# Fewer zero products around the last expert products, a first store on another queue, ten split rows for twelve

## The chip, the core and the metric

One core of a Trainium2 chip runs the whole kernel. The metric is the device time of one execution in microseconds; the figure of the kernel before is the median of 13 runs. The profile is one execution, seen by the hardware profiler: it gives the start and length of every instruction on TensorE (PE, with its weight loads as PEld), VectorE (DVE), ScalarE (ACT), GpSimd (POOL) and SyncE (SP), the packets of the 16 DMA engines, and the clock that TensorE was granted.

## What is computed

Two operations follow each other. Attention over q, k, v of shape (4, 8, 768, 64), where each head is either full causal or causal with 4 sink positions and a window of 64; its output, laid out as x of shape (3072, 512), goes into a soft mixture of experts (8 experts with 4 slots each):

```
x = attention(q, k, v).transpose(0, 2, 1, 3).reshape(3072, 512)
logits = x @ phi                                   # 3072 x 32
d = exp(logits) normalised over tokens;  c = exp(logits) normalised over slots
slot_input = d.T @ x                               # 32 x 512
slot_out[e] = relu(slot_input[e] @ w1[e]) @ w2[e]  # w1: 512 x 1024, w2: 1024 x 512, for 8 experts
out = c @ slot_out                                 # 3072 x 512, f32
```

The combine product at the end needs every expert's slot output, so no row of the output can be made before the last w2 is in.

## The kernel before

**The attention** is one loop over 16 pairs of heads (`for n in range(NP)`, L324). For pair n the loop issues six chunks of scores with their exponentials (`scores`, L158 to L170), transposes q and k of pair n+1 on TensorE (`transposes`, L139) and copies them out of PSUM (`evac`, q on DVE at L146, k on ACT at L149), and multiplies the probabilities of pair n-1 by v (`pvmm`, L191). The order on each engine is the order of the source, written out by hand; nothing is reordered by a scheduler.

**The loads** all go through one GpSimd queue, in source order: q and k (L110), v (L116), w1 and w2 (L130), and at the end w2 of expert 5 (L405), the left half of columns of w2 of expert 6 (L407), and then, in one loop at L421, w2 of expert 7 left, of expert 6 right and of expert 7 right. They convert f32 in HBM to bf16 in SBUF.

**The tail** (from L427) runs the experts. `second(e, xs)` (L508 to L515) multiplies the hidden rows of expert e by w2[e] for the left half (x = 0) or the right half (x = 1) of the 512 output columns, into two PSUM tiles `sp[0]` and `sp[1]`; that is eight products per half and expert. TensorE's order is: the 24 small products of the row sums (L532), `second(5)`, `second(6)` and `second(7)` for the left half, the left half of `slot_out` copied by DVE (L563), the left half of the first NL = 12 rows of the output, `second(6)` and `second(7)` for the right half, the right half of `slot_out` (L568), then twelve rows in full width and the right half of the first twelve. Row r here means one output row of each of the 128 partitions. `product` (L545 to L551) makes one such row: a product into one of four PSUM buffers, then a scaled copy to SBUF, by DVE for even r (L551) and by ACT for odd r (L549).

**The stores.** `half_rows` (L553 to L560) stores groups of finished half rows; the left ones go out on the GpSimd queue in groups of 2, 2, 4 and 4. The full rows are stored by SP at L576 (groups of 1, 1, 2, 4, 4), the right half rows by SP at L560 (4, 4, 4). SP has issued nothing since L253 when the stores begin. A half row is 1 KB per partition, a full row 2 KB.

**Zero products.** `keep_busy(t, count)` (L266 to L268) issues products of a tile of zeros into a bank that nobody reads: 128 x 512 each. There are 9 at the very start (L271), 2 after each of the first transposes (L299), 2 in each of three places of the first pair, and at the end 1 (L472), 4 (L534), 4 (L536), 4 (L538) and 3 (L566); some at L425 and L450 besides.

Of the kernel before, what the change touches and what calls it, by code (L numbers as in the profile page):

```python
# [10 lines left out]
F32 = mybir.dt.float32  # L11
# [27 lines left out]
def kernel(  # L39
# [13 lines left out]
    nc = tc.nc  # L53
    P = 128
# [3 lines left out]
    NE, DM, F = moe_w1.shape  # L58
# [16 lines left out]
    def single(shape, dt, name, tag=None):  # L75
        return singles.tile(shape, dt, name=name, tag=tag or name)
# [29 lines left out]
    def load_qk(pairs, which):  # L106
        b, h, c = pairs[0] // 4, 2 * (pairs[0] % 4), 2 * len(pairs)
        src, d = (q, qraw) if which == "q" else (k, kraw)
        t = raw.tile([P, len(pairs), S], BF16, tag="r" + which, name="r" + which)
        nc.gpsimd.dma_start(t, src[b, h:h + c].rearrange("(y h) (p s) d -> (h p) y (s d)", h=2, s=12))  # L110
        for x, n in enumerate(pairs):
            d[n] = t[:, x]

    def load_v(m):
        b, h = m // 2, 4 * (m % 2)
        nc.gpsimd.dma_start(vbs[m % 3].rearrange("p h j d -> p (h j) d")[:, :, :D],  # L116
                            v[b, h:h + 4].rearrange("h (j p) d -> p (h j) d", p=P))
# [8 lines left out]
    def w_load(upto):  # L126
        while wi[0] < min(upto, 2 * NE - 3):
            e = wi[0] % NE
            dst, src = ((w1s, w1v), (w2s, w2v))[wi[0] // NE]
            nc.gpsimd.dma_start(dst[e], src[e])  # L130
            wi[0] += 1

    def transposes(n, which):
        src = (qraw if which == "q" else kraw)[n]
        tp = trp.tile([P, 12, 64], BF16, tag="tr", name="tp" + which)
        for s in range(12):
            for hh in range(2):
                po = slice(64 * hh, 64 * hh + 64)
                nc.tensor.transpose(tp[po, s, :], src[po, 64 * s:64 * s + 64], ident[po, po])  # L139
        return tp  # L140

    def evac(n, which, tp):
        dst = qkT.tile([P, S], BF16, tag="T" + which, name="T" + which)
        o, i = dst.rearrange("c (p s) -> c p s", s=12), tp.rearrange("c s p -> c p s")
        if which == "q":
            nc.vector.tensor_copy(o, i)  # L146
            qT[n] = dst
        else:
            nc.scalar.copy(o, i)  # L149
            kT[n] = dst  # L150
# [7 lines left out]
    def scores(n, c):  # L158
        o, ln, parts = CHUNKS[c]
        sc = scp.tile([P, 2, 512], F32, tag="sc", name="sc")  # L160
        at = 0
        for j, i0, cnt in parts:
            for hh in range(2):
                po = 64 * hh
                nc.tensor.matmul(sc[:, hh, at:at + 128 * cnt], kT[n][po:po + 64, j * 128:(j + 1) * 128],  # L165
                                 qT[n][po:po + 64, i0 * 128:(i0 + cnt) * 128], start=True, stop=True)
            at += 128 * cnt
        if c == 0:
            pT[n] = ptp.tile([P, 2, NPT], BF16, tag="pT", name="pT")
        nc.scalar.activation(pT[n][:, :, o:o + ln], sc[:, :, :ln], ACT.Exp, scale=scale)  # L170
# [50 lines left out]
    def logits_exp(b):  # L221
        nc.scalar.activation(expT[:, b], lgs[b][:96], ACT.Exp, accum_out=colpart[:, b:b + 1])  # L222
# [43 lines left out]
    def keep_busy(t, count):  # L266
        for _ in range(count):
            nc.tensor.matmul(t, zero[:, :P], zero, start=True, stop=True)  # L268

    idle = pvp.tile([P, 512], F32, tag="pv", name="idle")  # L270
    keep_busy(idle, 9)  # L271
    V.tensor_single_scalar(ident, diff[:, :P], 0.0, op=ALU.is_equal)
    one_row = single([1, P], BF16, "one_row")
    V.memset(one_row, 1.0)
# [19 lines left out]
    def head_mask(h):  # L294
        V.tensor_scalar(msk[:, h], grade, thr[:, h:h + 1], None, op0=ALU.is_ge)

    for which in ("k", "q"):
        evac(0, which, transposes(0, which))
        keep_busy(idle, 2)  # L299
    for h in range(2):  # L300
        head_mask(h)
    def far_mask(n):
# [21 lines left out]
    for n in range(NP):  # L324
        if n == 0:
            load_qk([2], "q")
            load_qk([2], "k")
            load_v(1)
        elif n == 1:
            load_qk([3], "q")  # L330
            load_qk([3], "k")
        elif n == 2 or (n % 2 == 1 and n < 12):
            m = 2 if n == 2 else (n + 3) // 2
            load_qk([2 * m, 2 * m + 1], "q")
            load_qk([2 * m, 2 * m + 1], "k")
            load_v(m)
        w_load(1 + 5 * (n + 1) // 8)
        if n == 0:
            nc.gpsimd.dma_start(phi, moe_phi.rearrange("(do di) s -> di do s", di=P))
        b, r = n // 4 - 1, n % 4  # L340
        last = n - 1

        scores(n, 0)
        if n == 0:
            keep_busy(idle, 2)
        if n >= 1:
            for i in range(3):
                pvmm(last, i)
        if b >= 0 and r == 2:
            logits_mm(b, (0, 1, 2, 3))  # L350

        scores(n, 1)
        if b >= 0 and r == 2:
            logits_exp(b)
        if n >= 1:
            norm(last, 0)
        if n + 1 < NP:
            tq = transposes(n + 1, "q")
            evac(n + 1, "q", tq)
        mask(n, 0)  # L360
        if b >= 0 and r == 3:
            exp_tokens(b)

        scores(n, 2)
        if n == 0:
            keep_busy(idle, 2)
        if n >= 1:
            pvmm(last, 3)
        if n >= 2:
            x_transpose(n - 2)  # L370
        mask(n, 1)

        scores(n, 3)
        if n + 1 < NP:
            tk = transposes(n + 1, "k")
        mask(n, 2)

        scores(n, 4)
        if n == 0:
            keep_busy(idle, 2)  # L380
        if n + 1 < NP:
            evac(n + 1, "k", tk)
        if n >= 1:
            pvmm(last, 4)
        vfar(n)

        scores(n, 5)
        if n >= 1:
            pvmm(last, 5)
            norm(last, 1)  # L390
        if b >= 0 and r == 3:
            dispatch_mm(b)
            slot_sum(b)
        if n < 3:
            far_mask(n + 1)
            for h in (2 * n + 2, 2 * n + 3):
                head_mask(h)
        elif n == 3:
            setup_late()
# [22 lines left out]
    idle = scp.tile([P, 512], F32, tag="sc", name="idle")  # L422
# [44 lines left out]
    cs = bank(1, (P, 1))  # L467
# [1 line left out]
    rcol = small.tile([P, 1], F32, tag="rc", name="rcol")  # L469
    V.reciprocal(rcol, cs)  # L470
    V.tensor_scalar(emask, emask, rcol, None, op0=ALU.mult)
    keep_busy(idle, 1)  # L472
    hs = []
    for e4 in range(2):
        t = xp.tile([P, 2, 512], BF16, tag="xb", name="hs")
# [30 lines left out]
    idle = spt[1][:, 1]  # L506
# [24 lines left out]
        er.append(e)  # L531
        nc.tensor.matmul(rp[:, r:r + 1], e[:ES], ones[:ES], start=True, stop=True)  # L532
    V.reciprocal(rrow, rp)
    keep_busy(idle, 4)  # L534
    second(5, spread=True)
    keep_busy(idle, 4)  # L536
    second(6, (0,), spread=True)
    keep_busy(idle, 4)  # L538
    second(7, (0,), spread=True)


    NL = 12
    ov = out.rearrange("(p r) d -> p r d", r=24)

    def product(r, o, cs, t):  # L545
        op = bank(t, (P, cs.stop - cs.start))
        nc.tensor.matmul(op, er[r], slot_out[:, cs], start=True, stop=True)  # L547
        if r % 2:
            nc.scalar.activation(o, op, ACT.Copy, scale=rrow[:, r:r + 1])  # L549
        else:  # L550
            V.tensor_scalar(o, op, rrow[:, r:r + 1], None, op0=ALU.mult)  # L551

    def half_rows(cs, t0, groups, banks, eng):  # L553
        ots = [single([P, n, 256], F32, f"oh{t0 + x}", tag=f"w1_{t0 + x}") for x, n in enumerate((8, NL - 8))]
        r = 0
        for rows in groups:
            for _ in range(rows):
                product(r, ots[r // 8][:, r % 8], cs, banks[r % len(banks)])
                r += 1
            eng.dma_start(ov[:, r - rows:r, cs], ots[(r - 1) // 8][:, (r - rows) % 8:(r - 1) % 8 + 1])  # L560

    left, right, full = slice(0, 256), slice(256, 512), slice(0, 512)
    V.tensor_copy(slot_out[:, left], sp[0])  # L563
    half_rows(left, 0, (2, 2, 4, 4), (1, 2), nc.gpsimd)
    second(6, (1,), spread=True)
    keep_busy(idle, 3)  # L566
    second(7, (1,), spread=True)
    V.tensor_copy(slot_out[:, right], sp[1])  # L568
    r = NL
    for t, groups in enumerate(((1, 1, 2), (4,), (4,))):  # L570
        ot = single([P, 4, DM], F32, f"ot{t}", tag=f"w1_{4 + t}")
        for rows in groups:
            for _ in range(rows):
                product(r, ot[:, r % 4], full, (1, 2)[r % 2])
                r += 1
            nc.sync.dma_start(ov[:, r - rows:r, :], ot[:, (r - rows) % 4:(r - 1) % 4 + 1])  # L576
    half_rows(right, 2, (4, 4, 4), (1, 2), nc.sync)


# [33 lines left out]
```

## Time and profile before

| what | value |
|---|---|
| time, median of 13 runs | 160.6 us (158.83 to 163.75) |
| the profiled execution's own time | 160.6 us |
| its span, first to last instruction | 158.8 us |
| outside the span | 1.8 us |
| mean granted TensorE clock | 0.952 |
| busy: PE, DVE, ACT, POOL | 122.6, 107.7, 108.6, 40.5 us |
| read from HBM, written to HBM | 52.49 MB, 6.29 MB |
| last product (L547) ends, last scaled copy (L549) ends | 146.8, 147.3 us |

Times inside a profile are counted from the span's start. In the table of windows each row is one stretch of time: its length, the busy time of PE, PEld, DVE, ACT and POOL with the number of instructions in brackets, the granted TensorE clock (1.00 is full), the busy share of the DMA engines, and GB/s. These GB/s count bytes as they land: a weight is 4 bytes in HBM and 2 in SBUF. "DMA to landing" runs from the start of the issuing instruction to the moment when its semaphore says that all is there.

### The profile page before, as it was taken

To read this page: it belongs to the slowest core of one execution; us is meant where nothing else is said; L and a number is where in the kernel's file an instruction comes from. 1 tells how busy PE (TensorE), PEld (TensorE's weight loads), DVE (VectorE), ACT (ScalarE), POOL (GpSimd) and SP (SyncE) were. 2 spreads that over 40 slices of the span, in tenths; PEclk is the share of its full clock that TensorE was granted. 3 is DMA by queue.
4 is the path that set the end of the run, shared out by engine and by line. 5 is a ranking of instruction groups with operands and counts; after the bars stand their busy time and mean duration, and the time that the engine had idled before them with its cause. 6 is when DMAs were issued, how large, how long until landed. Compare 5 with 4: busy or idle time off the path is not lost. (4 is left out here: it accounts for less than half of the span.)

```text
span 158.8 us, 5124 instructions
## 1 busy us (share of the span) xinstructions
PE 122.6 (77%) x2272; PEld 75.1 (47%) x2272; DVE 107.7 (68%) x249; ACT 108.6 (68%) x147; POOL 40.5 (25%) x57
## 2 busy tenths in 40 slices
PE   6947679597697799897979977978879999778000
PEld 2422456365465565565655655655544753444000
DVE  6268599888986978977878977868655300769000
ACT  3248799769799989999998999897124310659100
POOL 7584153601330440340392000003600000420000
PEclk9999999969999999999999999999999987999955
DMA  3999999999999999999999999999999999299993
GB/s 51 161 175 202 172 224 197 195 191 187 218 215 200 188 217 199 188 212 200 195 211 194 203 206 229 204 225 204 227 208 216 189 200 166 68 302 398 396 344 101
DMA packets 38744, 32.87 MB, mean 207 GB/s; under 512 B 26050, under 2 KB 35778, under 8 KB 36802
## 3 DMA queue, kind: packets, MB, share of 16 engines
q0 software_dynamic: 36416, 27.82, 111.7%
q1 hardware_dynamic: 2306, 4.72, 8.0%
q8 instruction: 18, 0.29, 0.7%
q14 instruction: 4, 0.03, 0.1%
HBM read 52.49 MB, written 6.29 MB: 370 GB/s over the span
## 5 line engine op out<-in xcount | busy, mean ns | idle before, releaser
L170 ACT ACTIVATE pT<-sc 128x1024 bf16<-128x1024 f32 (+1 forms) x96 | 83.5, 924 | 10.5 <-PE sc L165 9.9
L165 PE MATMUL sc<-Tq,Tk 64*128 64x256 bf16 (+3 forms) x320 | 35.4, 283 | 12.1 <-ACT Tk L149 11.0
L191 PEld LDWEIGHTS <-pT 128*128 128x128 bf16 x672 | 24.3, 98 | 11.5 <-issue 6.9
L182 DVE TENSOR_TENSOR pT<-pT,msk 128x1024 bf16<-128x1024 bf16 (+1 forms) x48 | 29.2, 639 | 0.0
L191 PE MATMUL pv<-vb,pT 128*128 128x65 bf16 x352 | 26.9, 194 | 0.3 <-DVE xb L200 0.3
L191 PE MATMUL pv<-vf,pT 128*128 128x65 bf16 x320 | 24.8, 196 | 0.0
L165 PEld LDWEIGHTS <-Tk 64*128 64x128 bf16 x320 | 10.6, 94 | 21.7 <-ACT Tk L149 13.7
L146 DVE COPY Tq<-tpq 128x768 bf16<-128x768 bf16 x16 | 15.3, 957 | 7.2 <-PE tpq L139 6.9
L200 DVE TENSOR_TENSOR xb<-pv,rs 128x384 bf16<-128x384 f32 x32 | 17.8, 558 | 1.1
L149 ACT COPY Tk<-tpk 128x768 bf16<-128x768 bf16 x16 | 12.9, 809 | 4.1 <-PE tpk L139 4.1
L110 POOL DMA_DIRECT2D rq<-in_q_dram x10 | 6.4, 639 | 35.9 <-PE sc L165 34.2
L199 DVE RECIPROCAL rs<-pv 128x6 f32<-128x6 f32 x32 | 6.2, 194 | 10.2 <-PE pv L191 10.2
L116 POOL DMA_DIRECT2D vb<-in_v_dram x8 | 11.6, 1452 | 3.5 <-PE pv L191 3.5
L139 PE MATMUL tpq<-ident,rq 64*64 64x64 bf16 x384 | 9.2, 196 | 4.1 <-DMA rq<-in_q_dram 4.1
L139 PEld LDWEIGHTS <-rq 64*64 64x64 bf16 x384 | 7.4, 111 | 8.3 <-DMA rq<-in_q_dram 4.9
L549 ACT ACTIVATE oh<-bank,rrow 128x256 f32<-128x256 f32 x12 | 5.2, 472 | 8.6 <-PE bank L547 8.5
L139 PE MATMUL tpk<-ident,rk 64*64 64x64 bf16 x384 | 9.6, 200 | 1.0 <-DVE Tq L146 1.0
L139 PEld LDWEIGHTS <-rk 64*64 64x64 bf16 x384 | 7.9, 114 | 4.6 <-issue 4.6
L268 PE MATMUL idle<-zero 128*128 128x512 bf16 x24 | 9.1, 496 | 1.2 <-DVE zero L264 1.2
L208 PE MATMUL tpx<-ident,xb 128*128 128x128 bf16 x96 | 8.4, 224 | 2.0 <-ACT expT L222 1.1
L547 PE MATMUL bank<-slot_out,expR 128*128 128x256 bf16 (+1 forms) x36 | 7.8, 306 | 2.3 <-DVE slot_out L568 0.5
L209 DVE COPY xT<-tpx 128x768 bf16<-128x768 bf16 (+1 forms) x17 | 9.0, 529 | 0.7 <-PE tpx L208 0.6
(92 smaller groups left out, 127.1 us busy)
## 6 DMA issues: line engine op xcount, KB each, us to landing
w<-in_moe_w_dram POOLq DMA_DIRECT2D x13, 1024.0 KB, 18.3
w<-in_moe_w_dram POOLq DMA_DIRECT2D x6, 512.0 KB, 18.9
vb<-in_v_dram POOLq DMA_DIRECT2D x8, 384.0 KB, 13.2
rq<-in_q_dram POOLq DMA_DIRECT2D x6, 384.0 KB, 12.0
rk<-in_k_dram POOLq DMA_DIRECT2D x6, 384.0 KB, 12.2
out_dram<-ot SPq DMA_DIRECT2D x2, 1024.0 KB, 8.0
out_dram<-oh SPq DMA_DIRECT2D x3, 512.0 KB, 9.1
out_dram<-oh POOLq DMA_DIRECT2D x2, 512.0 KB, 4.3
```

Source lines behind the costliest of these rows:

```text
L116: nc.gpsimd.dma_start(vbs[m % 3].rearrange("p h j d -> p (h j) d")[:, :, :D], v[b, h:h + 4].rearrange("h (j p) d -> p (h j) d", p=P))
L139: nc.tensor.transpose(tp[po, s, :], src[po, 64 * s:64 * s + 64], ident[po, po])
L146: nc.vector.tensor_copy(o, i)
L149: nc.scalar.copy(o, i)
L165: nc.tensor.matmul(sc[:, hh, at:at + 128 * cnt], kT[n][po:po + 64, j * 128:(j + 1) * 128], qT[n][po:po + 64, i0 * 128:(i0 + cnt) * 128], s ...
L170: nc.scalar.activation(pT[n][:, :, o:o + ln], sc[:, :, :ln], ACT.Exp, scale=scale)
L182: nc.vector.tensor_mul(x, x, m)
L191: nc.tensor.matmul(pv[n][:, i % 3, hh, :], pT[n][:, hh, o:o + 128], vv[:, hh, j, :D + 1], start=(j == 0), stop=(j == i))
L200: nc.vector.tensor_mul(xb[b][:, 3 * half:3 * half + 3, h * D:(h + 2) * D].rearrange("p i (h d) -> p i h d", h=2), pv[n][:, :, :, :64], rs. ...
L208: nc.tensor.transpose(tp[:, i * 128:(i + 1) * 128], xb[b][:, i, hp * 128:(hp + 1) * 128], ident)
L209: nc.vector.tensor_copy(xT[:, hp, i0 * 128:i1 * 128], tp[:, i0 * 128:i1 * 128])
L268: nc.tensor.matmul(t, zero[:, :P], zero, start=True, stop=True)
```

## The change

- At the front: 7 zero products for 9, and none after the first transposes or inside the first pair (10 fewer there; the ones at L425 and L450 stay).
- At the end: the 1 of L472 and the 4 of L534 go; the 4 of L536 stay; of the 4 of L538 one stays; the 3 of L566, between the right halves of experts 6 and 7, go.
- The first of the left stores is issued by SP, the others by GpSimd as before.
- NL is 10. The left groups are 2, 2, 4, 2; the full-width rows are 14, in groups of 1, 1, 2, 4, 4, 2; the right groups are 4, 4, 2.

```diff
-    keep_busy(idle, 9)
+    keep_busy(idle, 7)
...
         evac(0, which, transposes(0, which))
-        keep_busy(idle, 2)
...
-        if n == 0:
-            keep_busy(idle, 2)
...
     V.tensor_scalar(emask, emask, rcol, None, op0=ALU.mult)
-    keep_busy(idle, 1)
...
     V.reciprocal(rrow, rp)
-    keep_busy(idle, 4)
     second(5, spread=True)
     keep_busy(idle, 4)
     second(6, (0,), spread=True)
-    keep_busy(idle, 4)
+    keep_busy(idle, 1)
     second(7, (0,), spread=True)
...
-    NL = 12
+    NL = 10
...
-    def half_rows(cs, t0, groups, banks, eng):
+    def half_rows(cs, t0, groups, banks, engs):
...
-            eng.dma_start(ov[:, r - rows:r, cs], ots[(r - 1) // 8][:, (r - rows) % 8:(r - 1) % 8 + 1])
+            engs[min(r > 2, len(engs) - 1)].dma_start(ov[:, r - rows:r, cs], ots[(r - 1) // 8][:, (r - rows) % 8:(r - 1) % 8 + 1])
...
-    half_rows(left, 0, (2, 2, 4, 4), (1, 2), nc.gpsimd)
+    half_rows(left, 0, (2, 2, 4, 2), (1, 2), (nc.sync, nc.gpsimd))
     second(6, (1,), spread=True)
-    keep_busy(idle, 3)
     second(7, (1,), spread=True)
...
-    for t, groups in enumerate(((1, 1, 2), (4,), (4,))):
+    for t, groups in enumerate(((1, 1, 2), (4,), (4,), (2,))):
...
-    half_rows(right, 2, (4, 4, 4), (1, 2), nc.sync)
+    half_rows(right, 2, (4, 4, 2), (1, 2), (nc.sync,))
```

More of the change, by code (lines that the diff above doesn't have):

```diff
@@ L364 @@
         scores(n, 2)
-        if n == 0:
-            keep_busy(idle, 2)
         if n >= 1:
@@ L378 @@
         scores(n, 4)
-        if n == 0:
-            keep_busy(idle, 2)
         if n + 1 < NP:
@@ L569 @@
     r = NL
-    for t, groups in enumerate(((1, 1, 2), (4,), (4,))):
-        ot = single([P, 4, DM], F32, f"ot{t}", tag=f"w1_{4 + t}")
+    for t, groups in enumerate(((1, 1, 2), (4,), (4,), (2,))):
+        ot, base = single([P, 4, DM], F32, f"ot{t}", tag=f"w1_{4 + t}"), r
         for rows in groups:
             for _ in range(rows):
-                product(r, ot[:, r % 4], full, (1, 2)[r % 2])
+                product(r, ot[:, r - base], full, (1, 2)[r % 2])
                 r += 1
-            nc.sync.dma_start(ov[:, r - rows:r, :], ot[:, (r - rows) % 4:(r - 1) % 4 + 1])
-    half_rows(right, 2, (4, 4, 4), (1, 2), nc.sync)
+            nc.sync.dma_start(ov[:, r - rows:r, :], ot[:, r - rows - base:r - base])
+    half_rows(right, 2, (4, 4, 2), (1, 2), (nc.sync,))
 _INS = ['q', 'k', 'v', 'is_retrieval', 'n_sink', 'window', 'moe_phi', 'moe_w1', 'moe_w2']
```

## Prediction

> **What bounds the kernel now.** I read the tail first, as windows of busy time with DMA rates:
>
> ```profile
> core 0: us, PE busy (x) PEld busy (x) DVE busy (x) ACT busy (x) POOL busy (x), PEclk, DMA share, GB/s
> 126.00:129.00 3.00, 2.92 (x44) 2.07 (x45) 0.42 (x1) 1.07 (x2) 0.00 (x0) 1.00 1.45 197
> ...
> 134.40:135.50 1.10, 0.88 (x11) 0.32 (x10) 0.17 (x1) 0.00 (x0) 0.00 (x0) 1.00 0.83 112
> 135.50:137.00 1.50, 0.94 (x6) 0.73 (x6) 1.14 (x4) 0.77 (x2) 0.00 (x0) 1.00 0.18 25
> 137.00:138.50 1.50, 1.40 (x15) 0.79 (x13) 1.50 (x4) 1.49 (x5) 1.29 (x2) 1.00 0.00 0
> 138.50:141.00 2.50, 1.97 (x20) 1.05 (x16) 0.97 (x3) 0.43 (x2) 1.65 (x3) 1.00 0.87 288
> 141.00:143.40 2.40, 2.03 (x8) 0.92 (x7) 2.40 (x5) 2.40 (x5) 0.00 (x0) 1.00 1.01 341
> 143.40:151.00 7.60, 2.87 (x14) 1.73 (x13) 3.83 (x8) 3.88 (x9) 0.00 (x0) 0.96 1.02 402
> 151.00:156.00 5.00, 0.00 (x0) 0.00 (x0) 0.00 (x0) 0.00 (x0) 0.00 (x0) 0.50 0.99 336
> ```
>
> Until about 134 the loads run unbroken at 200 GB/s landed (twice that read). Then comes a hole: the loads' last bytes trickle in until 137.0, and no store byte moves before 138.5. From there stores fill the engines to 156: 402 GB/s while full rows go, 336 at the end where half rows go. The last computing instruction ends at 147.3, so the end is set by when the stores begin and how many bytes are left, not by TensorE's last product.
>
> When each load lands, from the page of line L421:
>
> ```profile
> L421 POOL DMA_DIRECT2D w<-in_moe_w_dram x3: 873/873/883, 112.8 to 114.5; - x3
> ...
> DMA to landing us min/median/max: 18.9/20.7/22.5
> ```
>
> Issued at 112.8, 113.6 and 114.5 and landing in order: w2[7] left at 131.7, w2[6] right at 134.3, w2[7] right at 137.0. The chain of work that ended last says what the first store waited for:
>
> ```profile
> 129.57 1.39 PE bank L268 x4
> 130.96 0.99 PE bank L513 x16
> 131.95 1.70 PE bank L268 x4
> 133.65 0.33 PE bank L513 x8
> 133.98 0.97 PE bank L268 x4
> 134.95 0.36 PE bank L513 x8
> ...
> 138.28 0.33 PE bank L513 x8
> 138.61 0.76 PE bank L268 x3
> 139.37 0.36 PE bank L513 x8
> ```
>
> L268 are zero products. They hold back the left slot_out (135.34) by 4.1 us in all and the right one (139.75) by 0.8 more.
>
> **Part 1, zero products before the left half.** The four at 129.57 (1.39 us) go; four stay; three of the last four go. The granted clock was 0.50 from 130.0 to 133.4, and I assume the same stretch again, since the row sums before it stay. From 129.57: second(5) 0.75 (between 0.66, twice the 0.33 of eight at full clock, and 0.99), four zeros 1.70, second(6) 0.5, one zero 0.43 (a quarter of 1.70), second(7) 0.5 (both above their 0.33 to 0.36, being at half clock now). Sum 3.9: left slot_out at 133.4, 1.9 earlier. At full clock it would be 0.66 + 0.97 + 0.33 + 0.25 + 0.36 = 2.6, so 132.1. The load permits either: w2[7] left is in at 131.7.
>
> **Part 2, zero products between the right halves.** Ten left rows keep TensorE until about left slot_out + 2.5 (twelve: 135.34 to 138.28), so 135.9; second(6) right follows at 136.3, its weights in since 134.3. Then second(7) right would come at once, but its weights land at 137.0. The 0.76 us of zeros, and most of what part 1 gained, turn into a wait on that DMA. Queued behind it on TensorE are all right-hand products; behind those DVE, ACT and SP. It starts at 137.05 against 139.30: 2.25 earlier, instead of the 3.1 that TensorE's sum gives (1.9, 0.4 for two rows fewer, 0.8). Only if left slot_out comes after 134.2 does TensorE set the right side again.
>
> The Trainium skill speaks against removing zeros (TensorE: Matmul & The Clock Gate, Why this matters for your kernels): a pause of some 3 us drops the clock to half. The row first: the clock fell at 130.0 with the zeros in place. If it fell again after 136, eight second products take 0.5 for 0.36, and a right-hand row at half clock an estimated 0.43 us (a zero product of the same 512 columns took 1.70/4) against the 0.33 at which DVE and ACT make rows now (0.66 for two). 262 KB in 0.43 us is 610 GB/s, still above 402. By the rule I would lose up to 0.5 us, by the row nothing; I take nothing and keep 0.5.
>
> **Part 3, the first store on SP.** Its row was ready 1.87 after left slot_out (137.21), so 135.3 now, and rows 3 and 4 are ready for GpSimd at the same time instead of queueing 0.7 us behind it. Landing times, from the DMA issues:
>
> ```profile
> out_dram<-oh POOLq DMA_DIRECT2D x2, 256.0 KB, 2.7
> out_dram<-ot SPq DMA_DIRECT2D x2, 256.0 KB, 3.5
> ```
>
> By the row SP is 0.8 slower, though that one ran behind left stores. The skill (DMA: Bandwidth & Descriptors, Specifications) gives the hardware queue's first byte as 0.4 us sooner (0.6 against 1). GpSimd's first byte came 1.3 after issue (138.5). So left bytes begin at 136.2 by the rule and 137.4 by the row; I take 136.6, GpSimd's own figure, since its store starts at the same moment. SP has nothing queued before it and is free again by 137.2 even at 1.9 us for the issue, well before its next store. A loss is possible too: left stores can slow the last load bytes (25 GB/s after 135.5: under 40 KB), at most some 0.3.
>
> **Part 4, ten split rows.** Left bytes 10 x 131 KB = 1.31 MB: 2.5 us at 288, the rest at 341, 4.2 us, done at 140.8. Right: second(7) plus copy gate 0.45, slot_out at 137.5, first full-row store 1.68 later (139.75 to 141.43) at 139.2. Its bytes came 2.0 after issue before (143.4, where the rate jumps), at 141.2 now; the lower bound is the left stores' end, 140.8. Then 14 full rows, 3.67 MB at 402, 9.1 us, and ten half rows, 1.31 MB at 336, 3.9 us: 154.2, or 153.8. The same sum for before, 143.4 + 3.15/0.402 + 1.57/0.336 = 155.9, meets the table's 156. Gain 1.7 to 2.1; I take 1.9. Two more full rows cost 0.5 net in that stretch and are in the sum. SP's two extra issues are hidden: rows are computed by 145.2, nine us ahead of the end.
>
> **Part 5, the front.** Twelve zeros go, worth 0.3 to 0.5 us each on TensorE, but I cost them at nothing:
>
> ```profile
> PE tpq L139 <- DMA rq<-in_q_dram: 4.1, 3, 1.6
> ...
> 30.80 0.74 PE L139 MATMUL tpq<-ident,rq 64*64 64x64 bf16 x24 [1.22 <-DMA rq<-in_q_dram]
> ```
>
> From the waits and the timeline: TensorE waits for q three times, at 11.5, 18.4 and last at 30.8 for 1.22 us. What it gains before is lost there, and the loads do not wait for it. A colder clock costs only what exceeds that 1.22. The cold stretch 31.0 to 34.4 prices it: copies of Tk at 27.51 and 35.77 are 8.26 apart, less 1.22 of waiting and some 6.2 for a usual pair: 0.8 per 3.4 us. I take 0; bounds 0 to 5.6 (seven such stretches, 7.1 to 31). The one at L472 (0.38) lies beside the copy of siT and its wait: 0, at most 0.2 either way.
>
> **The rivals.** *The landing is not the end of it* (0.13): left stores flow from 136.2 by the rule and right bytes follow issue by 1.2 (a 64-byte load on SP landed in that time near the start), so there is no slow stretch: the left 1.31 MB take 3.3 us at 402 for the 4.2 above and the right ones follow without a hole, a further 1.0: 157.7. For: both queues feed at once. Against: the 288 of before.
> *The hardware queue is late, or left stores delay the last load* (0.13): right bytes 0.7 later and the left ones at 137.4, a second hole, plus 0.5 of cold clock: 160.0.
> *Cold front, slower* (0.12): without zeros TensorE stays at half clock from 7.1 to 31, seven stretches of 0.8 make 5.6 us late, less 1.2 of waiting at 30.8 and 0.8 until left slot_out passes 134.2; 3.6 remain on the right side, 162.3. It turns the sign from 1.2 + 0.8 + 1.9 us, or five cold stretches. For: transposes and short products keep TensorE only 60 to 70% busy there with zeros. Against: products at half clock fill the time, and a full window restored it at 34.4.
> *Forecast* (0.62): the wait for w2[7] right replaces the zeros.
>
> **Numbers.** The profiled execution took 160.6, 1.8 outside its span of 158.8, and equals the median of the runs; 160.6 - 1.9 = 158.7. Half a per cent (0.8 us) is about what a measurement can tell from no change. Faster by that: forecast nearly whole, and the first rival, 0.78; within, the second rival mostly, 0.11; slower 0.11. Range 157.3 to 160.4: from a little below the first rival, past the second.
>
> **What would show it.** Right: a wait of second(7) right on a DMA, 0.5 to 1 us, ending at 137; left slot_out near 133.4; store bytes from 136.6; an end of store bytes near 154; loads landing unchanged. Wrong: second(7) right after 138, a hole in store traffic after 140, a granted clock of 0.50 over most of 7 to 31, or w2[7] right landing later than 137.3.

## The result and the profile after

The changed kernel takes 157.73 us (median of 11 runs, 156.69 to 159.74); the kernel before, in its 48 runs by then, 160.97. The ratio is 0.9849, with a 95% interval of 0.9814 to 0.9885: 2.4 us less, between 1.8 and 3.0. (A ratio uses only the executions within 1.5% of their kernel's fastest, so it lies nearer to 1 than the quotient of two medians.) The two profiled executions differ by 3.4 us, spans of 158.8 and 155.4. The forecast was 158.7, 1.9 us less.

The windows of the kernel after, cut where those of before were cut, show the same columns: length, busy time of the five rows, granted clock, DMA share, GB/s.

```profile
126.00:129.00 3.00, 2.92 (x49) 2.01 (x42) 0.42 (x1) 1.07 (x2) 0.00 (x0) 1.00 1.45 198
134.40:135.50 1.10, 0.85 (x6) 0.66 (x6) 0.86 (x3) 0.75 (x2) 0.00 (x0) 1.00 1.08 147
135.50:137.00 1.50, 1.15 (x13) 0.62 (x12) 1.32 (x4) 1.41 (x4) 0.78 (x2) 1.00 0.69 193
137.00:138.50 1.50, 0.91 (x11) 0.64 (x11) 0.52 (x2) 0.00 (x0) 1.45 (x2) 1.00 0.61 212
138.50:141.00 2.50, 2.18 (x9) 1.12 (x8) 2.50 (x4) 2.37 (x4) 0.00 (x0) 1.00 0.96 329
141.00:143.40 2.40, 1.92 (x9) 1.09 (x8) 2.40 (x5) 2.40 (x5) 0.00 (x0) 1.00 1.03 397
143.40:150.00 6.60, 1.28 (x8) 0.68 (x6) 1.79 (x5) 1.84 (x5) 0.00 (x0) 0.76 1.01 404
150.00:153.50 3.50, 0.00 (x0) 0.00 (x0) 0.00 (x0) 0.00 (x0) 0.00 (x0) 0.50 1.04 346
153.50:154.00 0.50, 0.00 (x0) 0.00 (x0) 0.00 (x0) 0.00 (x0) 0.00 (x0) 0.50 0.46 152
```

The hole is filled: 193 and 212 GB/s stand where 25 and 0 stood. Between 135.5 and 143.4 the difference is 252 + 318 + 102 + 134 KB, together 0.81 MB, and at 384 GB/s, the mean of the rows from 143.4 to 153.5, that is 2.1 us. The store bytes end at 153.9, where I had 154.2 or 153.8.

TensorE around the two halves, after (start, length, operation; in brackets what it waited for):

```profile
129.69 1.05 PE L505 MATMUL bank<-w,hT 128*32 128x256 bf16 x16
130.67 1.89 PE L268 MATMUL bank<-zero 128*128 128x512 bf16 x4
132.49 0.62 PE L505 MATMUL bank<-w,hT 128*32 128x256 bf16 x8
133.04 0.43 PE L268 MATMUL bank<-zero 128*128 128x512 bf16 x1
133.40 0.40 PE L505 MATMUL bank<-w,hT 128*32 128x256 bf16 x8
...
136.33 0.40 PE L505 MATMUL bank<-w,hT 128*32 128x256 bf16 x8
137.07 0.40 PE L505 MATMUL bank<-w,hT 128*32 128x256 bf16 x8 [0.33 <-DMA w<-in_moe_w_dram]
```

The wait for w2[7] right is there, second(7) right starting at 137.07 (forecast 137.05). L505 is L513 of before. The landings of L414, L421 before, are hardly moved:

```profile
DMA to landing us min/median/max: 18.0/20.5/22.3
```

The last is issued at 114.7 and lands at 137.0, as before.

The other part of the profiles' difference is at the very end of the kernel before, in a row of its windows whose meaning I had not asked for:

```profile
156.00:157.00 1.00, 0.00 (x0) 0.00 (x0) 0.00 (x0) 0.00 (x0) 0.00 (x0) 0.50 0.09 30
```

Beside it stands the instruction queue's line (packets, MB, share) from the page of before and from the page of after:

```profile
q8 instruction: 18, 0.29, 0.7%
```

```profile
q8 instruction: 17, 0.28, 0.6%
```

Before, some 25 to 30 GB/s still trickle out from 156.0 to 157.2. A sixteenth of the stores' 336 to 402 GB/s is 21 to 25, and in the trace one store packet at a time is in flight from 156.1, where 16 and more were until 155.8; so it seems that one engine is still at work and the others are done. And the instruction queue moved 18 blocks of 16 KB, not 17. The packets behind these lines show the eighteenth at 146.9, a single packet of 0.92 us in the middle of the stores. After, there is no such block past 131.2, and the engines end together. The trace does not say which engine a packet ran on; that the late one is the one that carried the block is inferred, and the experiments below bear on it.

### The profile page after: what moved, and what is told of

The parts are those of the page before. It is cut to its first block, busy times and chain, and to the rows that moved or that the text cites. A ratio compares the mean times of both kernels' runs of the same rounds, so it can differ in the third digit from the quotient of the medians.

```text
span 155.4 us, 5076 instructions
## 1 busy us (share of the span) xinstructions
PE 119.5 (77%) x2247; PEld 75.3 (48%) x2247; DVE 108.2 (70%) x248; ACT 108.6 (70%) x146; POOL 39.8 (26%) x56
## 5 line engine op out<-in xcount | busy, mean ns | idle before, releaser
L165 PE MATMUL sc<-Tq,Tk 64*128 64x256 bf16 (+3 forms) x320 | 37.0, 298 | 12.9 <-ACT Tk L149 11.2
L191 PEld LDWEIGHTS <-pT 128*128 128x128 bf16 x672 | 24.8, 99 | 11.9 <-issue 6.9
L191 PE MATMUL pv<-vb,pT 128*128 128x65 bf16 x352 | 27.5, 196 | 0.3 <-DVE xb L200 0.3
L165 PEld LDWEIGHTS <-Tk 64*128 64x128 bf16 x320 | 11.2, 96 | 21.6 <-ACT Tk L149 13.9
L139 PE MATMUL tpq<-ident,rq 64*64 64x64 bf16 x384 | 10.2, 206 | 3.6 <-DMA rq<-in_q_dram 3.5
L139 PEld LDWEIGHTS <-rq 64*64 64x64 bf16 x384 | 8.3, 119 | 7.5 <-DMA rq<-in_q_dram 5.0
L538 PE MATMUL bank<-slot_out,expR 128*128 128x256 bf16 (+1 forms) x34 | 7.6, 315 | 2.3 <-DVE slot_out L554 0.5
L110 POOL DMA_DIRECT2D rk<-in_k_dram x10 | 6.6, 664 | 10.6 <-PE tpk L139 5.6
L540 ACT ACTIVATE oh<-bank,rrow 128x256 f32<-128x256 f32 x10 | 4.3, 472 | 6.9 <-PE bank L538 6.9
## 6 DMA issues: line engine op xcount, KB each, us to landing
w<-in_moe_w_dram POOLq DMA_DIRECT2D x13, 1024.0 KB, 18.2
```

Source lines behind the costliest of these rows:

```text
L191: nc.tensor.matmul(pv[n][:, i % 3, hh, :], pT[n][:, hh, o:o + 128], vv[:, hh, j, :D + 1], start=(j == 0), stop=(j == i))
```

## The experiments

Two theories after the first look. **Byte stream:** loads and stores are one stream over the DMA engines; the change gains what it takes out of that stream, the hole (2.1 us) and the late engine (1.1 us). **TensorE's chain** (rivals in several forms): what counts is when the first left store or the right half starts, and each zero product removed is worth its time.

In the code shown, "..." stands for lines that are the same in both, and a comment behind a line says where it stands.

**The tail's zeros alone.** The kernel before, less the eleven zero products that the change takes out of the tail:

```diff
-    keep_busy(idle, 1)      # after emask
...
-    keep_busy(idle, 4)      # before second(5)
...
-    keep_busy(idle, 4)      # before second(7) left
+    keep_busy(idle, 1)
...
-    keep_busy(idle, 3)      # between the right halves
```

> The kernel before, with nothing changed but the tail's zero products taken out as in the change (those of L472, L534, L566, three of L538). If the two waits on zeros were the whole gain, it takes nearly all of it: left slot_out near 133.9, second(7) right at about 137.05 just after its weights, store bytes from about 137.1, a time of 157.9 to 158.4, a ratio to before of 0.98 to 0.985. If the store's queue and the ten rows carry a real part, it keeps less than two thirds of the gain: 159 or more.

Measured: 158.93, ratio 0.9881 (0.9844 to 0.9917). Left slot_out at 133.24, first store byte at 136.5, second(7) right at 137.10; the store bytes end at 154.2, with no late engine. These zeros alone bring four fifths of what the change gains by the ratio, hole and late engine together, though the intervals of the two overlap; what the queue and the ten rows add is not settled by this.

**Three zeros between the right halves, put back** into the kernel after:

```diff
     second(6, (1,), spread=True)
+    keep_busy(idle, 3)
     second(7, (1,), spread=True)
```

> The kernel after, with the three zero products between second(6) right and second(7) right put back. They last 0.76 us, and in the kernel after TensorE waits 0.33 us there for w2[7] right, landing at 137.0. By the landing theory only the rest counts: second(7) right starts about 137.5 instead of 137.07, the time is 0.3 to 0.5 us longer, 158.1. By TensorE's sum (rival) it is 0.76 longer, 158.5.

Measured: 157.19, ratio 0.9831 (0.9797 to 0.9864). Not slower at all. TensorE with them in:

```profile
136.25 0.40 PE L505 MATMUL bank<-w,hT 128*32 128x256 bf16 x8
136.58 0.82 PE L268 MATMUL bank<-zero 128*128 128x512 bf16 x3
137.81 0.40 PE L505 MATMUL bank<-w,hT 128*32 128x256 bf16 x8 [0.40 <-DMA w<-in_moe_w_dram]
```

In this execution the weights landed 0.7 later than in the kernel after, and second(7) right started 0.74 later, held by them and not by the zeros; the store bytes still ended at 153.8. The trace shows why: the bytes of the first full-row store start at 140.80 (140.39 in the kernel after), and the left stores' bytes last until 140.94, so no gap opens. My expectation of 0.3 to 0.5 us failed, and with it the idea that the right half's start sets the end: it has slack.

**Eight zeros there,** to find the end of that slack in the same place:

```diff
     second(6, (1,), spread=True)
+    keep_busy(idle, 8)
     second(7, (1,), spread=True)
```

> The kernel after, with eight zero products between second(6) right and second(7) right (1.7 us at full clock). second(7) right starts at about 138.5 instead of 137.07, the first full-row store at 140.6. Three zeros there cost nothing. If the right side has slack as long as left bytes last, to about 140.5 plus the store's latency of some 1.5, this is past it: a hole of 0.7 to 1.4 us in the store bytes near 141 and 158.3 to 159.0. If the right side's start never matters (rival: the drain is all), 157.7.

Measured: 157.86, ratio 0.9848 (0.9791 to 0.9906). second(7) right at 139.43, and a dent appears in the window that follows, 254 GB/s where the kernel after has 397:

```profile
138.50:141.00 2.50, 1.93 (x15) 0.99 (x15) 0.65 (x2) 0.01 (x1) 0.88 (x2) 1.00 0.89 306
141.00:143.40 2.40, 2.07 (x7) 1.04 (x7) 2.40 (x4) 2.40 (x4) 0.00 (x0) 1.00 0.70 254
```

The dent is 0.34 MB, nine tenths of a microsecond, and there is a gap of half a microsecond between the last left byte (141.93) and the first full-row byte (142.40): here the slack has ended. But the median moves by 0.13, and the interval is too wide to find a price. The expected 158.3 to 159.0 was not met. The profile's store bytes end at 155.4, but that is not the zeros' price either: its loads ended 1.7 us later than in the kernel after (last load byte at 138.5 for 136.8).

**The left half in two stores,** to delay the first store alone:

```diff
-    half_rows(left, 0, (2, 2, 4, 2), (1, 2), (nc.sync, nc.gpsimd))
+    half_rows(left, 0, (8, 2), (1, 2), (nc.sync,))
```

> The kernel after, with the left half rows stored in two groups (8 and 2, both on SP) instead of four. TensorE, DVE and ACT do the same; the first store is issued some 1.4 us later, first byte at about 137.6 instead of 136.2. If the stores' first byte sets the end, store bytes end 1.0 to 1.4 us later: 158.7 to 159.1. If the right side's start sets it (my forecast's term), 157.7 within 0.4.

Measured: 157.38, ratio 0.982 (0.9764 to 0.9875). The first byte came at 137.0, 0.8 later than in the kernel after, and nothing was lost. Its windows:

```profile
135.50:137.00 1.50, 0.73 (x11) 0.37 (x10) 0.89 (x3) 0.98 (x3) 0.00 (x0) 1.00 0.51 69
137.00:138.50 1.50, 0.43 (x9) 0.29 (x9) 0.42 (x1) 0.00 (x0) 0.00 (x0) 1.00 1.03 344
138.50:141.00 2.50, 2.30 (x8) 1.12 (x8) 2.10 (x3) 1.53 (x3) 0.00 (x0) 0.71 1.04 347
```

The first bytes meet the last load bytes (landed at 137.5), and then the engines are full at once. That tells against "the first store byte sets the end", and against my forecast's term too, since second(7) right came at 137.54 and the bytes end at 153.8 again.

**No zeros before the left half** (the five that the change leaves there taken out):

```diff
     second(5, spread=True)
-    keep_busy(idle, 4)
     second(6, (0,), spread=True)
-    keep_busy(idle, 1)
     second(7, (0,), spread=True)
```

> The kernel after, with the last five zero products before the left half removed too. Left slot_out comes at about 132.0 instead of 133.85, the first store byte at about 134.4 instead of 136.2. If the gain was the hole between the last load bytes and the first store bytes, that hole is closed already: earlier stores share the engines with the loads' tail until 137, and the time stays at 157.7 within 0.5. If the end follows the first store byte by 17.7 us (rival; after: 136.2 to 153.9), it is 156.0. If the clock, with no zeros left, stays at half through the stores, slower than 158.2.

Measured: 157.07, ratio 0.9807 (0.9762 to 0.9851), the lowest of all full kernels, but its interval overlaps that of the change. In its profile the whole chain ran late, with 6.9 us at half clock from 42.7, and left slot_out came at 133.37 and not at 132.0; TensorE then waited 1.04 us for w2[7] right, and the bytes ended at 153.9. A lead of TensorE is lost in such a wait.

**One load less.** As the last, with this edit; the right half of the output then uses expert 5's columns for expert 6's:

```diff
-    for e, cs in ((7, slice(0, 256)), (6, slice(256, 512)), (7, slice(256, 512))):
+    for e, cs in ((7, slice(0, 256)), (7, slice(256, 512))):
...
+    w2s[6] = w2s[5]
     second(6, (1,), spread=True)
```

> As e6 (no zeros left before the left half), and the right half of w2 of expert 6 is not loaded; expert 5's columns stand in for it, so the right half of the output is another sum. The loads then end near 134.4 instead of 137.0, and so does w2[7] right. If loads and stores are one stream of bytes without a hole, all that the load took, up to 2.6 us, comes off, less what of it is a new hole before the first store byte at 134.4: 155.3 to 156.2. If the end hangs on TensorE's chain (rival), it equals e6.

Measured: 156.71, ratio 0.9788 (0.9741 to 0.9835). The loads ended at 134.7 as meant, but the stores did not follow:

```profile
133.00:134.70 1.70, 1.18 (x34) 1.02 (x24) 0.61 (x2) 0.00 (x0) 0.00 (x0) 0.88 0.31 46
134.70:136.40 1.70, 1.70 (x9) 1.08 (x7) 1.59 (x4) 1.37 (x4) 0.13 (x1) 0.50 0.00 0
136.40:141.00 4.60, 3.69 (x26) 1.91 (x27) 3.38 (x7) 2.93 (x7) 2.10 (x3) 0.86 0.84 287
```

A hole of 1.7 us is back: left slot_out came only at 133.88 (this execution had more stretches at half clock, one of them in the hole, from 134.3 to 137.7), and the first store byte at 136.40. Some 2.6 us less of loading brought 0.4 against the kernel without left zeros, and the intervals overlap. Expected was 155.3 to 156.2. In this one profile TensorE's chain is the bound again once the loads end sooner.

**The front's zeros,** put back into the kernel after:

```diff
-    keep_busy(idle, 7)
+    keep_busy(idle, 9)
...
+        keep_busy(idle, 2)      # after each of the first transposes
...
+        if n == 0:              # in three places of the first pair
+            keep_busy(idle, 2)
```

> The kernel after, with the front's zero products of before put back (9 at the start, 2 in each of the five places). If the front costs nothing (TensorE waits for q at 30.8 either way), the time is that of the kernel after within 0.4 us, some 157.7, and the clock is full from about 7 again. If the twelve zeros count (rival: TensorE's sum), it is 1 us or more slower, 158.7. If the cold front of the kernel after costs time (rival), it is faster by 0.5 us or more.

Measured: 157.84, ratio 0.9859 (0.9815 to 0.9902). No difference to be seen, as expected; the clock was not full from 7 on, though, but fell once more, from 12.4 to 15.8. TensorE's products number 2259 here, and no instruction block comes among the stores.

**The kernel before once more.**

> The kernel before, unchanged, for a second profile. In the first one the last store bytes trickled at 30 GB/s from 156.0 to 157.2, 1.2 us that the kernel after does not show. If that tail belongs to the kernel before, it is there again; if it was one execution's, the store bytes end within 0.4 us of the point where the rate falls below 300 GB/s.

Measured: 161.66 in its single run. The eighteenth instruction block is there again, at 147.9, and so is the late engine: from 157.4 one store packet at a time is in flight, until 158.2.

```profile
q8 instruction: 18, 0.29, 0.7%
```

```profile
155.50:157.00 1.50, 0.00 (x0) 0.00 (x0) 0.00 (x0) 0.00 (x0) 0.00 (x0) 0.50 1.05 348
157.00:158.30 1.30, 0.00 (x0) 0.00 (x0) 0.00 (x0) 0.00 (x0) 0.00 (x0) 0.50 0.22 76
```

**The front part of the change alone,** in the kernel before:

```diff
-    keep_busy(idle, 9)
+    keep_busy(idle, 7)
...
-        keep_busy(idle, 2)      # after each of the first transposes
...
-        if n == 0:              # in three places of the first pair
-            keep_busy(idle, 2)
```

> The kernel before with the front part of the change alone (twelve zero products fewer, before 16 us). In both profiles of the kernel before, one 16 KB transfer of the instruction queue runs for 0.9 us while the stores drain (at 146.9 and 147.9), and the store bytes of one DMA engine end about 1 us after those of the others; no profile with fewer TensorE instructions (2261 products or fewer for 2272) shows it. If the number of TensorE's instructions decides whether that fetch comes, it is gone here, with all else in the tail as before: about 1.0 us faster than before, a ratio near 0.994, and the store bytes end at once. If the front costs nothing and the late engine has another cause, 1.0 within its interval, and the late engine is there.

Measured: 160.33, ratio 0.9895 (0.9831 to 0.9958). This ratio rests on only four of the fourteen executions. The plain medians are 0.8 us apart (161.11 for the kernel before, run beside it), near the expected 1.0, but the two spreads overlap so far that the times alone do not settle it. The profile is clearer: the tail is that of before, left slot_out at 135.02, hole and all, but there is no instruction block among the stores, and the engines end together at 155.85, 17.7 us after the first store byte for 18.7 before.

```profile
q8 instruction: 17, 0.28, 0.6%
```

```profile
155.50:157.00 1.50, 0.00 (x0) 0.00 (x0) 0.00 (x0) 0.00 (x0) 0.00 (x0) 0.50 0.11 38
157.00:158.30 1.30, 0.00 (x0) 0.00 (x0) 0.00 (x0) 0.00 (x0) 0.00 (x0) 0.50 0.00 0
```

**Thirty zeros behind the last product** of the kernel after, for which nothing waits:

```diff
     half_rows(right, 2, (4, 4, 2), (1, 2), (nc.sync,))
+    keep_busy(idle, 30)
```

> The kernel after, with thirty zero products behind the last product of TensorE, for which nothing waits; they last some 6.5 us, from 145 to about 151.5, and end before the stores do. By the fetch theory TensorE's stream is again as long as before's (2277 products), the 16 KB instruction fetch comes during the stores and one engine ends about 1 us late: 158.6 to 158.9. By the rival (the fetch is no cost, or not TensorE's) 157.7 within 0.4.

Measured: 159.34, ratio 0.9922 (0.9888 to 0.9957): slower than the kernel after by 1.6 us in the medians and 1.2 by the ratios, with intervals that don't touch. The profiled execution was one of its longer ones (160.33; its last load byte came at 138.0), so only the order of events in it is used. The block is back, at 150.7 for 0.92 us; here are the queue's line on the page and the windows at the end:

```profile
q8 instruction: 18, 0.29, 0.7%
```

```profile
150.00:155.50 5.50, 2.54 (x12) 0.98 (x10) 0.00 (x0) 0.00 (x0) 0.00 (x0) 1.00 0.99 348
155.50:157.00 1.50, 0.00 (x0) 0.00 (x0) 0.00 (x0) 0.00 (x0) 0.00 (x0) 0.54 0.07 24
```

24 GB/s after 155.5 is about what one engine moves, until 157.0: 1.5 us behind the rest.

**The store's queue and the twelve rows,** one at a time in the kernel after:

```diff
-    half_rows(left, 0, (2, 2, 4, 2), (1, 2), (nc.sync, nc.gpsimd))
+    half_rows(left, 0, (2, 2, 4, 2), (1, 2), (nc.gpsimd,))
```

```diff
-    NL = 10
+    NL = 12
...
-    half_rows(left, 0, (2, 2, 4, 2), (1, 2), (nc.sync, nc.gpsimd))
+    half_rows(left, 0, (2, 2, 4, 4), (1, 2), (nc.sync, nc.gpsimd))
...
-    for t, groups in enumerate(((1, 1, 2), (4,), (4,), (2,))):
+    for t, groups in enumerate(((1, 1, 2), (4,), (4,))):
...
-    half_rows(right, 2, (4, 4, 2), (1, 2), (nc.sync,))
+    half_rows(right, 2, (4, 4, 4), (1, 2), (nc.sync,))
```

> The kernel after, with all left stores on the GpSimd queue. In the profile of the kernel after the first store byte came 0.9 us after the issue on SP, against 1.3 on GpSimd before. If only the right side's start sets the end, the time stays at 157.7 within 0.4. If the first store's start sets it (rival), the first bytes come 0.4 us later and the second and third store queue behind it by 0.7 us: 158.3 to 158.6.

> The kernel after with twelve split rows and their groups as before (left 2, 2, 4, 4; full 1, 1, 2, 4, 4; right 4, 4, 4). second(7) right is ready some 0.4 us later, inside or just past the wait for its weights, and four more half rows move 0.52 MB at 340 GB/s instead of 400: 0.2 to 0.4 us slower than after, 158.0. If more left bytes closed a hole (rival), 0.3 us faster.

Measured: 158.36, ratio 0.9893 (0.9844 to 0.9943), and 158.21, ratio 0.9877 (0.982 to 0.9934). They are slower than the change by 0.6 and 0.5 us. The first lies where I had put it if the first store's start sets the end, the second a little above what I expected; both intervals overlap that of the change, so neither is settled. In the first one's profile left slot_out was 0.9 late (134.78, at half clock from 132.1), and the first byte came 1.28 after its issue, at 138.0, 0.8 after the last load byte: a hole again, of which the queue's part can't be told apart.

## Why the prediction was right, point by point

**The mechanism held.** The end is set by when stores begin and by the bytes left; zeros at the left turn into a wait for w2[7] right; the loads don't move. The profile of the kernel after shows all three, though the wait was 0.33 us where I had said 0.5 to 1. The tail's gain came out at 2.1 us from the rates, and at 2.2 from the point where the bulk of the store bytes ends (156.1 to 153.9), against 1.7 to 2.1.

**Luck in the number.** The forecast of 1.9 us lies within the measured 1.8 to 3.0, but its sum lacked a term of 1.1 us in the profiles (the late engine, below). The first rival's 157.7 came nearer to the time.

**Zeros before the left half.** Left slot_out at 133.85, not 133.4: second(5) took 0.98 for 0.75, the four zeros 1.82 for 1.70, and the row sums ended 0.2 later. The cold stretch came again, 129.7 to 133.2. The new drop of the clock after 136, to which I had given up to 0.5 us, did not show in this profile (1.00 until 143.4). In three variants it did: at half clock were left in two stores from 139.5 to 142.9, front zeros back from 138.7 to 142.1, and no left zeros from 138.3 to 141.7. Their store bytes still ended at 153.7 to 153.9, so taking nothing for it was right.

**Zeros between the right halves.** The wait was 0.33, not some 0.75, because the left half came later. I said TensorE sets the right side from a left slot_out of 134.2; a wait of 0.33 with left slot_out at 133.85 puts that point at 134.18.

**A step that failed: the right side's bytes as the last term.** I took 2.0 us from the first full-row store's issue to its bytes, 141.2, and let the end hang on that, with the left stores done at 140.8. In the kernel after the issue is at 139.19 and the bytes start at 140.39, 1.2 later, as the first rival had it, while left bytes last until 141.23: there is no gap, and so nothing hangs on the right bytes' start. The rate in between was 329 GB/s from 138.5 to 141.0, between my 288 and the rival's 402. With three zeros put back second(7) right started 0.74 later at no cost, and with the left stores joined the left side's bytes began 0.8 later at no cost.

What stands in its place is the stream, and the fourteen profiles agree on it. In nine of them store bytes begin before the last load byte (the kernel after and all variants of it but two, and the tail's zeros alone). From the last load byte to the end of the store bytes, a late engine set aside, these nine take 16.3 to 17.5 us. In the other five the stores begin after it, and the hole adds about its own length:

| profile | hole, us | last load byte to end, us | less the hole |
|---|---|---|---|
| store on GpSimd | 0.8 | 18.2 | 17.3 |
| front only | 1.5 | 19.1 | 17.7 |
| before | 1.9 | 19.4 | 17.6 |
| one load less | 2.0 | 19.8 | 17.7 |
| before again | 2.5 | 20.1 | 17.6 |

**The front, costed at nothing.** As time on TensorE that is right, though it was colder than before, in part as my slower rival had it. Transposes of q in the kernel after:

```profile
11.33 0.85 PE L139 MATMUL tpq<-ident,rq 64*64 64x64 bf16 x24 [2.21 <-DMA rq<-in_q_dram]
...
18.20 0.85 PE L139 MATMUL tpq<-ident,rq 64*64 64x64 bf16 x24
...
24.43 0.56 PE L139 MATMUL tpq<-ident,rq 64*64 64x64 bf16 x24
...
30.97 0.85 PE L139 MATMUL tpq<-ident,rq 64*64 64x64 bf16 x24 [0.77 <-DMA rq<-in_q_dram]
```

They take 0.85 us where 0.56 is usual until the clock rose at 20.5, and the wait at 30.8 shrank from 1.22 to 0.77: it absorbed the loss. But as instructions the zeros were not free, the tail's no more than the front's: either set taken out alone, and the block is gone from the profile. That term was missing from my sum: one instruction block among the stores, 1.1 us in the profiles. I took the end of before as 155.9, "meets the table's 156", and left the row of 30 GB/s behind it unexplained. With 2.1 and 1.1 the profiles' 3.4 is nearly whole; the 2.4 us by the ratio is less than their sum, so how the gain of a usual execution divides is not known so closely.

**The store on SP.** First byte 0.9 us after the issue, against 1.3 on GpSimd. This is the kernel after from 135.2 to 137.3, in 40 slices of 0.0525 us:

```profile
GB/s 127 127 127 107 146 107 107 88 98 68 78 39 20 20 10 20 10 10 146 215 341 400 351 361 322 302 312 341 400 332 332 371 254 117 59 20 39 20 20 20
```

Issued at 135.25, its bytes rise in the nineteenth slice, at 136.15. The 0.4 us of difference by the cited rule came out, and the row I set against it (0.8 slower to landing, behind other stores) was of another situation. I was wrong on rows 3 and 4: they were not ready with the first two, and GpSimd issued them at 136.12, 0.9 later.

**Still open:** what the queue and the ten rows are worth by themselves, and what TensorE's lead would bring with fewer loads. No variant with the right output beats the change by more than the intervals.

## What to carry over

Where loads run to the end and stores drain after them, draw the bytes per microsecond first: in these runs a hole between the two was worth about its length, and once it was closed neither earlier nor slightly later arithmetic moved the end. Look at the last rows too: a rate that fits one DMA engine suggests that one of them was held up, and by what is a question to ask before the sum is made. Count instructions as well as time when fillers go in or out.

## What the runs showed of the hardware

Instructions come by DMA as well, in blocks of 16 KB on a queue of their own, each a single packet of about 0.9 us. The Trainium skill (Runtime: NRT & Kernel Launch, Instruction fetch mechanics) says that an engine's instructions are refilled in 16 KiB blocks of 256 instructions and that crossing a boundary is mostly hidden. The block size agrees. The cost was not hidden where a block fell among the stores: one engine ended 0.8 to 1.5 us after the others in the three profiles that have such a block (before, before again, thirty zeros), and neither block nor late engine stands in the other eleven.

The trace does not name the block's owner, but counts point to TensorE. Over the first seventeen blocks, TensorE starts 255 instructions per block in the kernel before and 257 in the kernel after, where VectorE starts some 13. The eighteenth comes at three different times, 146.9, 147.9 and 150.7, but each time when TensorE has started about the same number of recorded instructions: 4552, 4547 (five products are missing from that trace) and 4549. No other profile holds more than 4533. So the kernel before passed that point by a handful of instructions.
